# Whole-tile attention in three passes, 1e-9 on ScalarE, low weight halves on VectorE

## The chip, the cores and the metric

The kernel runs on one core of one Trainium2 chip. The core has five engines with a queue each: TensorE (PE in the profile, with its weight loads as PEld), VectorE (DVE), ScalarE (ACT), GpSimd (POOL) and SyncE (SP, which issues DMAs). An engine takes its instructions in the order in which they were written into its queue, and an instruction that waits holds those behind it. The metric is the device time of one execution in microseconds.

## What is computed

Three parts follow each other. Attention with a window: 4 batches, 8 heads, 768 positions, head size 64; a query in a chunk of 32 sees 16 positions to the left of the chunk, 8 to the right, and 8 memory positions. Then a gated product, and then a mix of 8 experts with balanced weights:

```python
scores = scale * np.matmul(q_c, k_full.transpose(0, 1, 3, 2))
scores = scores - np.max(scores, axis=-1, keepdims=True)
a = np.exp(scores)
a = a / (np.sum(a, axis=-1, keepdims=True) + 1e-09)
out[:, :, c_start:c_end] = np.matmul(a, v_full)
...
x = (x @ w_a) * (x @ w_b) @ w_out          # 3072 tokens, 512 -> 1536 -> 512
...
P = exp(logits - max); 8 times: rows, then columns of P scaled to sum 1 (columns to N / E)
for e in range(E):
    h = np.maximum(x @ w1[e], 0.0)
    out += P[:, e:e + 1] * (h @ w2[e])
```

## The kernel before, in words

**Precision.** A product is made of three: each operand is split into a high half (rounded to fp32r, by an ACT copy) and a low half (operand less high half). `mm3` multiplies low by high, high by low and high by high into one PSUM bank. Scores, transposes and values of attention are plain fp32 products; each of them stands in the trace with two records (of transposes, with one).

**First stage.** Tokens are in four passes of 768 (eight tiles of 96 queries), so a pass has 8 tiles of attention. A tile has two groups of four heads. For a group, `attn_group` adds: scores (PE, L408), masking with the scale (DVE, L417), negative maxima (DVE, L423), four exponentials with their sums (ACT, L426), the 1e-9 (DVE, L432), the reciprocal (DVE, L435), the product with it (POOL, L438, called the norm here), four transposes (PE, L445), a copy (ACT, L449), values (PE, L455), and the split of the result into `xbig` (ACT L463, DVE L466).

A pass has 12 steps of the gated product, two for each of six weight blocks: `product` makes `pab` (12 products of 128x384, L268), `second` makes `po` (6 of them). Attention of a pass is spread by its due times over the steps of the pass before; only the first pass's attention stands at the start with nothing beside it but the first weights. At the end of a pass come the logits: `pr`, a copy on ACT, and `folded` (`pl`).

**Weights.** Six blocks of six parts (128x512) are read in each of four passes, 144 parts in all. In the first pass the parts are made from 64-bit words on DVE (`d_clamp`, `d_shift`, `d_top`, `d_low`, L225 to L243). In every pass a part's high half is made by ACT (`w_high`, L257) and its low half by POOL (`w_low`, L261). Beside passes 2 to 4, weights of the expert stage are prepared: sums and splits on DVE in `dbuf`, `pbuf` and `xbig` (L277 in the trace, the helper `sub`), and stores from ACT's queue.

**The order.** `Order` holds a list of operations: engine, a cost, a due time, a function and what it comes after. `emit` runs them through a plan of its own: on each engine the ready operation with the lowest due time goes next, and the plan's times come from the costs. An engine name `DVE+` and the engine `POOL` share one port in this plan, so they exclude each other there. The order in which `emit` calls the functions is the order in every queue; the chip does not change it.

**Second stage.** The experts, from about 770 us to the end, with an order made in the same way.

## Time and profile before

| what | value |
| --- | --- |
| median of 3 runs | 2655.18 us (2654.46 to 2659.0) |
| the profiled execution | 2651.62 us, span 2649.7 us |
| PE, PEld busy | 2599.3 us (98%), 2218.6 us (84%) |
| DVE, ACT, POOL busy | 2122.5 us (80%), 1059.4 us (40%), 449.4 us (17%) |
| first stage to 760 us: PE, DVE, ACT, POOL busy | 729.7, 581.2, 422.6, 283.1 us |

The span runs from the first to the last instruction. A busy share is a mean over stages with different limits. Matmuls are pipelined and their ends are modelled, so on PE the distance from start to start tells more than a duration. In a row of a timeline several equal instructions are merged (x12); a bracket gives the idle time in front of it and what ended it.

### The profile page before, as it was taken

How to read it: one execution, taken by the hardware profiler on the slowest of the kernel's cores; microseconds unless marked ns; L12 is line 12 of the kernel's file. 1: busy time of each engine (PE TensorE's matmuls, PEld its weight loads, DVE VectorE, ACT ScalarE, POOL GpSimd, SP SyncE). 2: the span in 40 equal slices, each digit the busy share in tenths (PEclk: the TensorE clock that was granted, in tenths of full speed). 3: DMA queues.
4: the chain of work that ended last, by engine and by line, in shares of the span. 5: the costliest groups of instructions: out<-in, count | busy, mean ns of one | idle time of the engine just before them, and what ended most of it. 6: DMA issues, size and time to landing. Idle time of an engine off the chain costs nothing.

```text
span 2649.7 us, 35892 instructions
## 1 busy us (share of the span) xinstructions
PE 2599.3 (98%) x13067; PEld 2218.6 (84%) x13067; DVE 2122.5 (80%) x3093; ACT 1059.4 (40%) x1922; POOL 449.4 (17%) x270
## 2 busy tenths in 40 slices
PE   6999999999999999999999999999999999999998
PEld 5899989999987888888877888888887888888887
DVE  8985777886758999999997687777789587777777
ACT  7654655555425333333333322222233332323222
POOL 4443433333304222222210000000000000000000
PEclk8999999999999999999999999999999999999999
DMA  7654778778554666666676766666676766666663
GB/s 242 204 179 132 280 250 292 249 253 326 195 175 160 219 216 232 226 232 212 237 268 196 210 200 203 203 201 199 194 216 213 222 200 201 201 192 202 202 187 112
DMA packets 224079, 565.05 MB, mean 213 GB/s; under 512 B 21232, under 2 KB 41712, under 8 KB 219808
## 3 DMA queue, kind: packets, MB, share of 16 engines
q1 hardware_dynamic: 190112, 445.31, 54.1%
q10 hardware_dynamic: 33792, 117.44, 11.6%
q8 instruction: 105, 1.72, 0.3%
q14 instruction: 70, 0.57, 0.1%
HBM read 423.12 MB, written 139.56 MB: 212 GB/s over the span
## 4 chain that ended last, share of the span: by engine, by line
PE 91%; DVE 5%; DMA 2%; issue 1%; ACT 1%; POOL 0%; SPq 0%; ACTq 0%; DVEq 0%; POOLq 0%
PE py L268 25%; PE pa L268 19%; PE px L268 14%; PE pab L268 14%; PE po L268 7%; PE pr L268 7%; DMA wc<-xbig 1%; PE s_ps L408 1%; DVE xbig L277 1%; PE o_ps L455 1%; DVE sums L277 1%; PE t_ps L445 1%; DVE raw_e L277 0%; DMA abuf<-in_kw 0%; DVE hb L277 0%
## 5 line engine op out<-in xcount | busy, mean ns | idle before, releaser
L268 PE MATMUL py<-xbig,wbig 128*128 128x512 f32 x3168 | 802.3, 391 | 7.8 <-DVE sums L277 4.1
L268 PEld LDWEIGHTS py<-xbig,wbig 128*128 128x128 f32 x3168 | 594.7, 188 | 136.8 <-DVE sums L277 7.7
L1015 ACT ACTIVATE xbig<-hb 128x1024 fp32r<-128x1024 f32 x336 | 356.1, 1061 | 635.8 <-PE py L268 467.0
L268 PE MATMUL pa<-xbig,wbig 128*128 128x512 f32 x2304 | 586.3, 390 | 0.3 <-DVE xbig L277 0.3
L268 PEld LDWEIGHTS pa<-xbig,wbig 128*128 128x128 f32 x2304 | 431.4, 188 | 90.0 <-DVE xbig L277 0.9
L277 DVE TENSOR_TENSOR xbig<-hb,xbig 128x1024 fp32r<-128x1024 f32 x336 | 414.1, 1234 | 92.0 <-ACT xbig L1015 91.8
L277 DVE TENSOR_TENSOR sums<-py,sums 128x512 f32<-128x512 f32 x495 | 339.2, 686 | 164.1 <-PE py L268 157.9
L268 PE MATMUL px<-xbig,wbig 128*128 128x512 f32 x1728 | 441.9, 391 | 1.8 <-DVE part L277 1.1
L268 PE MATMUL pab<-xbig,wbig 128*128 128x384 f32 x2304 | 439.5, 339 | 1.7 <-DVE lg L606 1.6
L268 PEld LDWEIGHTS pab<-xbig,wbig 128*128 128x128 f32 x2304 | 401.6, 189 | 10.0 <-issue 3.5
L268 PEld LDWEIGHTS px<-xbig,wbig 128*128 128x128 f32 x1728 | 322.9, 188 | 70.5 <-DVE part L277 4.2
L937 ACT ACTIVATE part<-pa 128x512 f32<-128x512 f32 x192 | 114.8, 598 | 389.2 <-PE pa L268 388.2
L277 POOL TENSOR_TENSOR wbig<-raw_e,wbig 128x768 fp32r<-128x768 f32 (+1 forms) x56 | 166.3, 2970 | 448.4 <-ACT wbig L293 326.8
L268 PE MATMUL po<-gh,wbig 128*128 128x384 f32 x768 | 233.4, 346 | 2.2 <-ACT acc L581 2.2
L277 DVE TENSOR_TENSOR hb<-hb,hb 128x1024 f32<-128x1024 f32 x192 | 232.1, 1217 | 1.0
L951 DVE SCALAR_TENSOR_TENSOR hb<-part,pb 128x512 f32<-128x512 f32 x276 | 224.0, 815 | 2.6
L268 PE MATMUL pr<-xbig,wbig 128*128 128x512 f32 x864 | 218.8, 391 | 0.0
L268 PEld LDWEIGHTS pr<-xbig,wbig 128*128 128x128 f32 x864 | 162.9, 189 | 33.8
L277 DVE TENSOR_TENSOR part<-px,part 128x512 f32<-128x512 f32 x192 | 131.8, 686 | 38.7 <-PE px L268 36.0
L261 POOL TENSOR_TENSOR wbig<-raw_e,wbig 128x512 fp32r<-128x512 f32 x96 | 133.1, 1405 | 110.4 <-ACT wbig L257 102.4
L268 PEld LDWEIGHTS po<-gh,wbig 128*128 128x128 f32 x768 | 142.0, 189 | 8.3 <-ACT acc L581 2.4
L583 DVE TENSOR_TENSOR acc<-po,acc 128x384 f32<-128x384 f32 x160 | 88.7, 554 | 65.6 <-PE po L268 64.8
(126 smaller groups left out, 2157.5 us busy)
## 6 DMA issues: line engine op xcount, KB each, us to landing
wbig<-wc SPq DMA_DIRECT2D x336, 512.0 KB, 3.9
wbig<-wc SPq DMA_DIRECT2D x476, 256.0 KB, 3.5
wc<-xbig ACTq DMA_DIRECT2D x36, 1792.0 KB, 8.4
wc<-wbig ACTq DMA_DIRECT2D x28, 1792.0 KB, 7.7
raw_e<-w_f SPq DMA_DIRECT2D x72, 256.0 KB, 5.7
raw_e<-in_w_ex SPq DMA_DIRECT2D x28, 512.0 KB, 5.0
pb<-pT SPq DMA_DIRECT2D x23, 512.0 KB, 5.7
dbuf<-in_w_moe SPq DMA_DIRECT2D x18, 512.0 KB, 4.6
```

The source lines that it names most:

```text
L261: nc.gpsimd.tensor_tensor(out=wl, in0=raw(part), in1=f32(wh), op=ALU.subtract)
L268: nc.tensor.matmul(out=out, lhsT=a, rhs=b, start=first and i + j == 0, stop=last and i == n - 1 and j == 2, skip_group_check=skip,)
L277: (engine or nc.vector).tensor_tensor(out=out, in0=a, in1=b, op=op)
L408: nc.tensor.matmul(out=s_banks[:TQ, j % 2, 2 * g + j // 2, :], lhsT=qps[i % NQ][a:a + 64, (h0 + j) // 2, :], rhs=kts[i][a:a + 64, (h0 + j) ...
L445: nc.tensor.transpose(r["t_ps"][:, j, :], r["s"][:, j, :], ident[:TQ, :TQ])
L455: nc.tensor.matmul(out=r["o_ps"][a:a + 64, j // 2, :], lhsT=vts[i][:, h0 + j, :], rhs=r["pt"][:, 2 * (j % 2) + j // 2, :], start=True, sto ...
L583: nc.vector.tensor_tensor(out=a, in0=r["o", d], in1=a, op=ALU.add)
L937: "ACT", 0.6, at + 0.05, lambda: nc.scalar.activation(out=parts[j], in_=src, func=AF.Copy),
L951: y = add("DVE", 0.69, due, lambda: nc.vector.scalar_tensor_tensor(out=dst, in0=src, scalar=0.0, in1=pb[:, j * HB:(j + 1) * HB], op0=ALU.m ...
L1015: "ACT", 1.05, d, lambda: nc.scalar.activation(out=h, in_=src, func=AF.Copy), *deps, *t_used.get(t_n - NTR, ()))
```

## The change

Four edits. `w_low` moves from GpSimd to VectorE. The addition of 1e-9 moves from VectorE to ScalarE, as an activation with a bias from a small tile (`tiny`). Attention of passes 2 to 4 (24 tiles) is no longer by groups but by `attn_tile`: scores of all eight heads at once, one addition and one reciprocal for eight heads, one PSUM tile and one split for the values of eight heads, and values of a tile in one operation (`both`) with the scores of the next tile; only the last tile of a pass has values alone. And the folded logits get a later due time and their copy a higher cost in the plan.

```diff
@@ -137,6 +137,7 @@
     st1 = const.tile([P, E], F32, name="st1")
     mrow = const.tile([1, P], F32, name="mrow")
     mx = const.tile([P, 1], F32, name="mx")
+    tiny = const.tile([P, 1], F32, name="tiny")
 
     gate = const.tile([P, KT, 32], F32, name="gate")
     fold = const.tile([P, E], F32, name="fold")
@@ -258,7 +259,7 @@
 
     def w_low(i, part):
         wh, wl = w_halves(i, part)
-        nc.gpsimd.tensor_tensor(out=wl, in0=raw(part), in1=f32(wh), op=ALU.subtract)
+        nc.vector.tensor_tensor(out=wl, in0=raw(part), in1=f32(wh), op=ALU.subtract)
 
     def mm3(out, pairs, first=True, last=True, skip=False):
 
@@ -429,7 +430,7 @@
                 )
 
             def sums():
-                nc.vector.tensor_scalar_add(r["sm"], r["sm"], 1.0e-9)
+                nc.scalar.activation(out=r["sm"], in_=r["sm"], func=AF.Identity, bias=tiny[:TQ])
 
             def inverses():
                 nc.vector.reciprocal(r["sm"], r["sm"])
@@ -468,7 +469,7 @@
             scored[x] = add("PE", 0.6, due, scores, qk_loaded, scored.get(x - 1), taken.get(x - 2))
             taken[x] = y = add("DVE", 0.6, due, masked, scored[x], turned.get(x - 4))
             y = add("DVE", 0.6, due, maxima, y)
-            y = add("DVE+", 0.07, due, sums, *[add("ACT", 0.39, due, lambda j=j: exps(j), y) for j in range(4)])
+            y = add("ACT", 0.2, due, sums, *[add("ACT", 0.39, due, lambda j=j: exps(j), y) for j in range(4)])
             y = add("DVE", 0.1, due, inverses, y)
             y = add("POOL", 1.02, due, norm, y)
             turned[x] = add("PE", 0.34, due, transposes, y, turned.get(x - 1), copied.get(x - 1))
@@ -477,6 +478,118 @@
             y = highs_x[x] = add("ACT", 0.22, due, high, valued[x])
             settled[x] = add("DVE", 0.28, due, low, y)
 
+        held = []
+
+        def attn_tile(i, qk_loaded, v_loaded, due):
+            t = i % NT
+            mask = masks[0 if t == 0 else 2 if t == NT - 1 else 1]
+            x = 2 * i
+            r = {}
+
+            def scores():
+                for g in range(2):
+                    for j in range(4):
+                        a = 64 * (j % 2)
+                        nc.tensor.matmul(
...
+            def masked(g):
...
+            def sums():
+                nc.scalar.activation(out=r["sm"], in_=r["sm"], func=AF.Identity, bias=tiny[:TQ])
+
+            def inverses():
+                nc.vector.reciprocal(r["sm"], r["sm"])
+
+            def norm(g):
...
+            def values():
...
+            def settle():
+                y = highs_x[x] = highs_x[x + 1] = add("ACT", 0.42, due, high, valued[x])
+                settled[x] = settled[x + 1] = add("DVE", 0.47, due, low, y)
+
+            before = [scored[x - 1], taken[x - 2], taken[x - 1], qk_loaded]
+            if held:
+                values_before, settle_before, v_before = held.pop()
+
+                def both():
+                    values_before()
+                    scores()
+
+                y = add("PE", 2.1, due, both, *before, copied[x - 2], copied[x - 1], v_before, settled[x - 3])
+                valued[x - 2] = valued[x - 1] = y
+                settle_before()
+            else:
+                y = add("PE", 1.2, due, scores, *before)
+            scored[x] = scored[x + 1] = y
+            done = []
+            for g in range(2):
+                y = taken[x + g] = add("DVE", 0.6, due, lambda g=g: masked(g), scored[x], turned[x + g - 4], turned[x - 3])
+                y = add("DVE", 0.6, due, lambda g=g: maxima(g), y)
+                done += [add("ACT", 0.39, due, lambda g=g, j=j: exps(g, j), y) for j in range(4)]
+            y = add("ACT", 0.2, due, sums, *done)
+            y = inverted = add("DVE", 0.1, due, inverses, y)
+            for g in range(2):
+                y = add("POOL", 1.02, due, lambda g=g: norm(g), inverted)
+                turned[x + g] = add(
+                    "PE", 0.34, due, lambda g=g: transposes(g), y, turned[x + g - 1], copied[x + g - 1])
+                copied[x + g] = add("ACT", 0.55, due, lambda g=g: copies(g), turned[x + g], valued[x + g - 2] if x + g - 2 in valued else None)
+            if (i + 1) % TILES_A_PASS:
+                held.append((values, settle, v_loaded))
+            else:
+                valued[x] = valued[x + 1] = add(
+                    "PE", 0.95, due, values, copied[x], copied[x + 1], v_loaded, settled[x - 1])
+                settle()
+
+        TILES_A_PASS = SB // TQ
         GB = 2 * NB // TQ
         qk_in, v_in = {}, {}
         for x in range(2 * len(tiles)):
@@ -491,7 +604,10 @@
             if g == 0:
                 qk_in[i] = add("SP", 1.5, due - EARLY, lambda i=i: qk_load(i), scored.get(x - 2 * NQ + 1))
                 v_in[i] = add("SP", 0.5, due - EARLY + 0.1, lambda i=i: v_load(i), valued.get(x - 2 * NV + 1))
-            attn_group(x, i, g, qk_in[i], v_in[i], due)
+            if i < TILES_A_PASS:
+                attn_group(x, i, g, qk_in[i], v_in[i], due)
+            elif g == 0:
+                attn_tile(i, qk_in[i], v_in[i], due)
 
 
         highs, lows, stored, first_used, second_used = {}, {}, {}, {}, {}
@@ -520,7 +636,7 @@
 
                 used = (first_used if p * DN < n_parts(i) * DN - NF * D else second_used).get(i - 2, ())
                 highs[i, p] = add("ACT", 0.52, due, lambda p=p: w_high(i, p), y, *used)
-                lows[i, p] = add("POOL", 1.23, due, lambda p=p: w_low(i, p), highs[i, p], *used)
+                lows[i, p] = add("DVE+", 0.6, due, lambda p=p: w_low(i, p), highs[i, p], *used)
 
         gated = add("SP", 0.5, 4.0, lambda: nc.sync.dma_start(
             out=gate[:, :, 0:E], in_=w_gate.rearrange("(k p) e -> p k e", p=P)))
@@ -642,9 +758,9 @@
                 y = z = add("PE", 0.7, x + 1, logits, *seconds[-1:], *free_po[-2:-1], *mine, gated)
                 finished[n, k] = (stored_x[n, k], y)
                 seconds.append(y)
-                y = add("ACT", 0.4, x + 1, rows_copy, y)
+                y = add("ACT", 0.6, x + 1, rows_copy, y)
                 free_po.append(y)
-                y = add("PE", 0.6, x + 1, folded, *free_po[-2:-1], y)
+                y = add("PE", 0.6, x + 1.6, folded, *free_po[-2:-1], y)
                 seconds.append(y)
                 z = add("DVE", 0.15, x + 1, lg_copy, y)
                 free_po.append(z)
@@ -709,6 +825,7 @@
                     nc.vector.memset(halves[32 * c:32 * c + 32, :, lo:hi], 0.0)
             make_identity(nc, ident)
             nc.vector.memset(ones, 1.0)
+            nc.vector.memset(tiny, 1.0e-9)
 
             nc.vector.memset(gate, 0.0)
             nc.vector.reduce_sum(
```

The order of PE in the second pass. `o_ps` are values, `s_ps` scores, `t_ps` transposes, x4 four heads; `pab` and `po` are the gated product. Before:

```order
L268 MATMUL pab<-xbig,wbig 128x384 x12
L455 MATMUL o_ps<-pt,abuf 64x96 x4
L268 MATMUL po<-gh,wbig 128x384
L268 MATMUL po<-gl,wbig 128x384
L268 MATMUL po<-gh,wbig 128x384 x2
L268 MATMUL po<-gl,wbig 128x384
L268 MATMUL po<-gh,wbig 128x384
L408 MATMUL s_ps<-abuf 96x128 x4
L268 MATMUL pab<-xbig,wbig 128x384 x12
L445 MATMUL t_ps<-ident,s_sb 128x96 x4
```

After, the same engine in the same pass:

```order
L269 MATMUL pab<-xbig,wbig 128x384 x12
L531 MATMUL t_ps<-ident,s_sb 128x96 x4
L269 MATMUL po<-gh,wbig 128x384
L269 MATMUL po<-gl,wbig 128x384
L269 MATMUL po<-gh,wbig 128x384 x2
L269 MATMUL po<-gl,wbig 128x384
L269 MATMUL po<-gh,wbig 128x384
L269 MATMUL pab<-xbig,wbig 128x384 x12
L542 MATMUL o_ps<-pt,abuf 64x96 x8
L493 MATMUL s_ps<-abuf 96x128 x8
```

Values of four heads and scores of four heads were two visits; values of one tile and scores of the next, eight heads each, are now one.

The order of POOL at the start, norms (`s_sb`) and low halves (`wbig`). Before:

```order
L438 TENSOR_TENSOR s_sb<-s_sb,sm 96x512 x4
L261 TENSOR_TENSOR wbig<-raw_e,wbig 128x512
L438 TENSOR_TENSOR s_sb<-s_sb,sm 96x512
L261 TENSOR_TENSOR wbig<-raw_e,wbig 128x512
L438 TENSOR_TENSOR s_sb<-s_sb,sm 96x512
L261 TENSOR_TENSOR wbig<-raw_e,wbig 128x512 x2
L438 TENSOR_TENSOR s_sb<-s_sb,sm 96x512 x2
```

After:

```order
masks.py:199 AFFINE_SELECT ident<-ident 128x128
L439 TENSOR_TENSOR s_sb<-s_sb,sm 96x512 x16
L524 TENSOR_TENSOR s_sb<-s_sb,sm_896 96x512 x2
L524 TENSOR_TENSOR s_sb<-s_sb,sm_1135 96x512 x2
L524 TENSOR_TENSOR s_sb<-s_sb,sm_1388 96x512 x2
```

POOL's queue of the first stage holds norms alone now: 16 of the first pass, then two for each tile.

The order of DVE in the start: maskings (L417, after: L418), maxima (L423, L424), the 1e-9 (L432, gone), reciprocals (L435, L436), the making of the weights, the split of attention (L466, L467). Before:

```order
L229 TENSOR_SCALAR raw_e<-raw_e 128x512
L435 RECIPROCAL sm<-sm 96x4
L236 SCALAR_TENSOR_TENSOR raw_e<-dbuf,raw_e 128x512
L432 TENSOR_SCALAR sm<-sm 96x4
L435 RECIPROCAL sm<-sm 96x4
L243 SCALAR_TENSOR_TENSOR raw_e<-dbuf,raw_e 128x512
L466 TENSOR_TENSOR xbig<-o_ps,xbig 128x2x96
L432 TENSOR_SCALAR sm<-sm 96x4
L435 RECIPROCAL sm<-sm 96x4
L417 SCALAR_TENSOR_TENSOR s_sb<-s_ps,abuf 96x512
```

After:

```order
L230 TENSOR_SCALAR raw_e<-raw_e 128x512
L436 RECIPROCAL sm<-sm 96x4
L237 SCALAR_TENSOR_TENSOR raw_e<-dbuf,raw_e 128x512
L244 SCALAR_TENSOR_TENSOR raw_e<-dbuf,raw_e 128x512
L436 RECIPROCAL sm<-sm 96x4
L467 TENSOR_TENSOR xbig<-o_ps,xbig 128x2x96
L262 TENSOR_TENSOR wbig<-raw_e,wbig 128x512
L418 SCALAR_TENSOR_TENSOR s_sb<-s_ps,abuf 96x512
```

The additions left the queue, and a low half (L262) stands in it, in front of a masking.

## Rows read from the trace of the kernel before

**Rows 1.** Busy time by stretches: from:to, length, busy us (count) by engine, clock, DMA.

```profile
47.00:75.00 28.00, 25.23 (x209) 21.36 (x208) 27.29 (x60) 24.44 (x87) 13.44 (x11) 0.98 0.78 245
75.00:350.00 275.00, 275.00 (x1844) 254.79 (x1843) 211.12 (x418) 156.13 (x439) 111.91 (x84) 1.00 0.61 202
...
sum 760.00, PE 729.67 PEld 679.43 DVE 581.23 ACT 422.57 POOL 283.05; mean PE 72.97 PEld 67.94 DVE 58.12 ACT 42.26 POOL 28.30
```

**Rows 2.** Waits of PE, 75 to 760 us: who for whom, us, times, longest.

```profile
PE o_ps L455 <- ACT pt L449: 3.0, 2, 2.5
PE po L268 <- ACT acc L581: 2.2, 1, 2.2
PE pab L268 <- DVE lg L606: 1.6, 1, 1.6
PE po L268 <- DVE gl L568: 0.7, 1, 0.7
```

**Rows 3.** Timeline of PE, two visits of attention: start, us, what.

```profile
336.33 2.25 PE L268 MATMUL pab<-xbig,wbig 128*128 128x384 f32 x12
338.41 0.49 PE L445 MATMUL t_ps<-ident,s_sb 96*128 96x96 f32 x4
338.69 0.42 PE L268 MATMUL po<-gh,wbig 128*128 128x384 f32 x1
338.94 0.34 PE L268 MATMUL po<-gl,wbig 128*128 128x384 f32 x1
...
339.64 0.34 PE L268 MATMUL po<-gh,wbig 128*128 128x384 f32 x1
339.91 0.68 PE L408 MATMUL s_ps<-abuf 64*96 64x128 f32 x8
340.52 0.55 PE L455 MATMUL o_ps<-pt,abuf 128*64 128x96 f32 x8
341.00 2.35 PE L268 MATMUL pab<-xbig,wbig 128*128 128x384 f32 x12
343.19 0.33 PE L268 MATMUL po<-gh,wbig 128*128 128x384 f32 x1
```

**Rows 4.** The stretch 25 to 50 us, and scores of eight and four heads in it.

```profile
25.00:50.00 25.00, 16.58 (x114) 12.77 (x114) 22.39 (x50) 19.13 (x70) 14.63 (x11) 0.59 0.68 222
...
28.84 2.03 PE L408 MATMUL s_ps<-abuf 64*96 64x128 f32 x16
...
32.30 1.17 PE L408 MATMUL s_ps<-abuf 64*96 64x128 f32 x8
```

**Rows 5.** Busy time by stretches of the low halves (L261) alone.

```profile
0.00:75.00 75.00, 14.35 (x11) 0.86 0.76 243
...
sum 760.00, POOL 200.22; mean POOL 100.11
```

**Rows 6.** DVE to 760 us: groups (busy, mean ns), lines L568 and L277 (min/median/max).

```profile
L568 DVE TENSOR_TENSOR gl<-a_sb,gh 128x384 fp32r<-128x384 f32 x94 | 67.1, 717 | 13.1 <-ACT gh L565 12.8
L277 DVE TENSOR_TENSOR xbig<-dbuf,xbig 128x512 fp32r<-128x512 f32 x54 | 44.6, 843 | 6.0 <-ACT xbig L293 5.9
...
L568 DVE TENSOR_TENSOR gl<-a_sb,gh x94: 519/552/4064, 62.8 to 748.5; 128x384 fp32r<-128x384 f32 x94
...
L277 DVE TENSOR_TENSOR xbig<-dbuf,xbig x74: 410/680/1809, 254.6 to 730.3; 128x512 fp32r<-128x512 f32 x54, 128x256 fp32r<-128x256 f32 x18, 128x1024 fp32r<-128x1024 f32 x2
```

**Rows 7.** Busy time by stretches of the 1e-9 (L432) alone.

```profile
0.00:75.00 75.00, 5.03 (x17) 0.86 0.76 243
75.00:760.00 685.00, 10.23 (x48) 1.00 0.66 228
```

**Rows 8.** ACT to 760 us, groups of the exponentials.

```profile
L426 ACT ACTIVATE s_sb<-s_sb,nm 96x128 f32<-96x128 f32 x256 | 99.5, 391 | 42.1 <-DVE nm L423 42.1
...
L426 ACT ACTIVATION_READ_ACCUMULATOR s_sb<-s_sb,nm 96x1 f32 x256 | 48.3, 189 | 0.0
```

**Rows 9.** Idle time of PE in front of the values (L455), by what ended it.

```profile
  ACT pt L449: 13.0, 12
```

More of the change, by code (lines that the diff above doesn't have):

```diff
@@ L478, in attn_group, with maxima, exps, transposes @@
             settled[x] = add("DVE", 0.28, due, low, y)
+        held = []
[9 more added lines that the diff above has]
+                        nc.tensor.matmul(
+                            out=s_banks[:TQ, j % 2, 2 * g + j // 2, :], lhsT=qps[i % NQ][a:a + 64, (4 * g + j) // 2, :],
+                            rhs=kts[i][a:a + 64, (4 * g + j) // 2, :], start=True, stop=True,
+                        )
+            def masked(g):
+                if g == 0:
+                    r["nm"] = sp.tile([TQ, 8], F32, tag="nm8", name="nm8", bufs=2)
+                    r["sm"] = sp.tile([TQ, 8], F32, tag="sm8", name="sm8", bufs=2)
+                s = r["s", g] = sp.tile([TQ, 4, TK], F32, tag="s_sb", name="s_sb", bufs=4)
+                nc.vector.scalar_tensor_tensor(
+                    out=s.rearrange("p (b r) k -> p b (r k)", b=2),
+                    in0=s_banks[:TQ, :, 2 * g:2 * g + 2, :].rearrange("p b r k -> p b (r k)"), scalar=SCALE,
+                    in1=mask[:, None, :].to_broadcast([TQ, 2, 2 * TK]), op0=ALU.mult, op1=ALU.add,
+                )
+            def maxima(g):
+                nc.vector.tensor_reduce(out=r["nm"][:, 4 * g:4 * g + 4], in_=r["s", g], axis=AX.X, op=ALU.max, negate=True)
+            def exps(g, j):
+                s = r["s", g][:, j, :]
+                c = 4 * g + j
+                nc.scalar.activation(out=s, in_=s, func=AF.Exp, bias=r["nm"][:, c:c + 1], accum_out=r["sm"][:, c:c + 1])
+            def sums():
[3 more added lines that the diff above has]
+            def norm(g):
+                nc.gpsimd.tensor_tensor(
+                    out=r["s", g], in0=r["s", g], in1=r["sm"][:, 4 * g:4 * g + 4, None].to_broadcast([TQ, 4, TK]), op=ALU.mult
+                )
+            def transposes(g):
+                r["t", g] = ps.tile([P, 4, TQ], F32, tag="t", name="t_ps")
+                for j in range(4):
+                    nc.tensor.transpose(r["t", g][:, j, :], r["s", g][:, j, :], ident[:TQ, :TQ])
+            def copies(g):
+                r["pt", g] = sp.tile([P, 4, TQ], F32, tag="pt", name="pt", bufs=2)
+                nc.scalar.activation(out=r["pt", g], in_=r["t", g], func=AF.Copy)
+            def values():
+                r["o"] = ps.tile([P, 4, TQ], F32, tag="o", name="o_ps")
+                for g in range(2):
+                    for j in range(4):
+                        a = 64 * (j % 2)
+                        nc.tensor.matmul(
+                            out=r["o"][a:a + 64, 2 * g + j // 2, :], lhsT=vts[i][:, 4 * g + j, :],
+                            rhs=r["pt", g][:, 2 * (j % 2) + j // 2, :], start=True, stop=True,
+                        )
+            here_h, here_l = (x1(y, slice(0, 4), i * TQ, TQ) for y in range(2))
+            def high():
+                nc.scalar.activation(out=here_h, in_=r["o"], func=AF.Copy)
+            def low():
+                nc.vector.tensor_tensor(out=here_l, in0=r["o"], in1=f32(here_h), op=ALU.subtract)
+            def settle():
[20 more added lines that the diff above has]
+            y = inverted = add("DVE", 0.1, due, inverses, y)
+            for g in range(2):
+                y = add("POOL", 1.02, due, lambda g=g: norm(g), inverted)
[8 more added lines that the diff above has]
+                settle()
```

## The prediction

> **What bounds the kernel now.** I read the busy time by stretches first, then the waits of PE, then PE's timeline, and last the groups of DVE and POOL. The stretches [rows 1] show a start in which DVE is close to full (27.3 of 28.0 us between 47 and 75), and behind it a stretch in which PE is busy without a gap (275.0 of 275.0) while DVE has 211 and ACT 156. The reader should not trust a busy PE alone, since its ends are modelled; so the second view is what PE waited for between 75 and 760 us, nearly the end of the first stage [rows 2]. It is 7.5 us in all, in five waits: 3.0 for the copies of attention, 2.2 for a copy of a sum, 1.6 for the logits and 0.7 for a split. So in this stage the time is the sum of what PE is given, and whatever is taken from PE's queue shortens the run as long as nothing new makes PE wait. All that the change touches lies there; the expert stage behind it issues the same work.
>
> The third view is how PE's queue runs through a visit of attention, from start to start [rows 3]. Twelve undisturbed products of `pab` take 338.41 - 336.33 = 2.08 us, so 0.17 each. Transposes of four heads take 0.28 us (338.41 to 338.69), and the product behind them 0.25 instead of 0.17: 0.08 more. In the next visit, scores and values: the last `po` before it takes 0.27 instead of 0.17 (339.64 to 339.91), scores of four heads 0.61, values of four heads 0.48, and the twelve `pab` behind 2.19 instead of 2.08. Going into and coming out of such a visit thus costs 0.10 + 0.11 = 0.21 us beyond its content, however much is in it.
>
> **The change, part by part.**
>
> *Attention by whole tiles, on PE.* In the built orders of PE I counted the unbroken runs of attention or logits products between expert products, from the first `pab` on: 133 before, 92 after. Those with scores or values in them fall from 89 to 33, those of transposes alone rise from 34 to 48. The number of products is the same. Switching: 56 x 0.21 = 11.8 us less, 14 x 0.08 = 1.1 us more, so 10.7 us less. Inside the runs there is a second gain: 24 have scores of eight heads and 25 values of eight heads. No row shows eight heads at the full clock, but the start has both lengths of scores where the granted clock is near the lower level (0.59 on the mean of its stretch) [rows 4]: the second four heads add 2.03 - 1.17 = 0.86 us. At twice the clock that is 0.43 instead of 0.61, so 0.18 x 24 = 4.3 us. For the values I take the same ratio, 0.70 of 0.48, so 0.14 x 25 = 3.5 us. The ends of this part: nothing for the longer runs (10.7 us in all), or the values gain as much as the scores (0.18 each, 19.5 us). I take 10.7 + 4.3 + 3.5 = 18.5 us, since rows 4 are the only ones of that length.
>
> By the Trainium skill, page TensorEngine Tiling (Array Packing), section Tiling Modes, a change of tiling mode, not only of the tile, drains TensorE, and the turn from values to scores inside the new visit is such a change. If it cost another 0.10 us there, the sum would be some 2 us smaller. The turn from scores to values in rows 3 lies within the 0.61 us, so the trace speaks for leaving it out.
>
> *The low halves of the weights, from POOL to DVE.* There are 144, and they take 200.2 us of POOL, 1.39 each [rows 5]. On DVE the nearest row is the same subtraction in the same shapes for the expert weights: mean 843 ns, median 680 [rows 6]. The mean lies over the median because some run to 1.8 us, and for `gl` to 4.1 us; such a long one holds PE in the 0.7 us of rows 2. I read these as DVE losing time beside POOL. Mean less median, times count: `gl` 94 x 0.165 = 15.5 us, `xbig<-dbuf` 54 x 0.163 = 8.8, so 24 us in two groups of many. Of POOL's 283.1 us the low halves are 71%, so at least 17 us of these two go. Added: 144 x 0.68 = 98 us. Gone from DVE besides: the 1e-9, 15.3 us [rows 7], and in 24 tiles one of two reciprocals and part of a split (an estimate of 8 us). Net at most 98 - 17 - 15 - 8 = +58 us; at the other end each low half frees as much of DVE as it adds, and the net is 23 us less. Even at the worst DVE goes from 581 to 639 of 760 us. It lies beside PE: between 75 and 350 us DVE has 64 us free. I put nothing on PE for it, and take off the 0.7 us for `gl`. If this cover is gone, it is in the start. What queues behind: a low half waits for ACT's high half and holds DVE's queue until then, as it now holds POOL's, where the norms stand behind it.
>
> *The start.* Eleven low halves stood in the first 75 us on POOL: 11 x 0.68 = 7.5 us more on DVE, 5.0 us of 1e-9 less [rows 5, 7], and relief between 17/144 = 0.12 and 0.68 us for each low half, 1 to 7.5 us. That is +1 to -5, or +4.3 with the 0.843 of the mean and no relief. I take 0.
>
> *The 1e-9 on ACT.* 40 small instructions, 16 by group and 24 by tile. The nearest row is the reading of an accumulator, 189 ns [rows 8]: 7.6 us on an engine busy 423 of 760. In the chain it takes the place of a DVE instruction of 15.3/64 = 0.24 us. Nothing, between -1 and +1.
>
> *The later due time of the folded logits.* It puts more in front of them; 1.6 us were waited for them in one place. I take 1 us less, between 0 and 1.6.
>
> *New waits.* PE's order now holds values of one tile and scores of the next as one block. If the values are late, the scores and all expert products behind wait too. Between this block and the first transposes of the next tile stand three `po` and three `pab`, 3 x 1.04 + 3 x 2.08 = 9.4 us. The tile's chain in that time: two maskings and two maxima of 0.68 like the row of that length, of which two are ahead of the first exponential (1.4 us), eight exponentials of at most 0.39 + 0.19 (4.6), the addition and the reciprocal 0.2 each, the norm (283.1 - 200.2)/64 = 1.3: 7.7 us. So 1.7 us are left for other work in the queues of DVE and ACT. I take 2 us of waits over all tiles; the ends are 0 and 26 (below).
>
> *Sum.* -18.5 - 0.7 - 1 + 2 = -18.2 us. On the profiled execution, 2651.62 us with a span of 2649.7, that is 2633.4. It lies 3.6 us under the median of the runs shown (2655.18), and I put the difference on the median: 2637 us.
>
> **The rivals.**
>
> *The block waits (slower).* Between a tile's last copy and its values. When PE waited for such a copy it was 12 times and 13.0 us, 1.1 us each [rows 9], most of it in the start. If each of the 24 tiles does so once, 26 us come in place of the 2 I took: 2637 + 24 = 2661 us. It decides from 25.5 us over 24 tiles, 1.06 us a tile (18.2 + 2 + the 5.3 us of 0.2%). For it: the slack of 1.7 us, and ACT's queue that held the copies up to 3.0 us in two places. Against it: only these two waits are left after 75 us [rows 2], in an order packed as closely.
>
> *Only the switches are saved.* The long runs cost what two short ones do, and the start is 4.3 us longer: 2655.2 - 10.7 + 4.3 - 1.7 + 2 = 2649 us; without the longer start 2645. For it: no row of eight heads at the full clock, and DVE without room in the start. Against it: rows 4, and the relief.
>
> *The gain goes into waits for ACT.* ACT's copies held PE 3.0 + 2.2 us in three places [rows 2]. A tile's chain is now longer and may meet every such hold: with five more of 3 us each, 2637 + 15 = 2652 us. Against it: nothing in the change makes ACT later but 7.6 us of small instructions.
>
> **How the numbers follow.** The forecast has 0.64, the switches alone 0.18, the block that waits 0.10, the holds of ACT 0.08. The forecast's own range is 2631 to 2643: 5 us better in the start and 1 of waits less, or 6 us of the long runs not there. The range for 8 of 10 goes down to 2630 and up to 2650, past the switches alone. A change within 0.2% (5.3 us, 2649.9 to 2660.5) is about what cannot be told from none. Faster: the forecast, the switches alone nearly whole, and a third of the holds, 0.84. Within 0.2%: the rest of these and a third of the waiting block, 0.08. Slower: 0.08.
>
> **What would show it.** In PE's timeline a visit of values and scores of eight heads each takes 0.34 + 0.48 + 0.43 + 0.61 = 1.9 us and 0.21 beyond; at 2.4 in all the longer runs gain nothing. The first stage ends some 18 us earlier with PE as full as before. On DVE the low halves take 0.68 us, and `gl` and the splits have means near their medians. PE's waits behind 75 us stay under 10 us. I am wrong if values or transposes stand high among them, if DVE fills the first 200 us and PE waits for its splits, or if the start is over 4 us longer.

## The result and the profile after

| | before | after |
| --- | --- | --- |
| median of the comparison | 2657.09 us (2654.46 to 2661.84) | 2625.54 us (2624.67 to 2630.01) |
| ratio, 95% interval | | 0.9888 (0.9876 to 0.99) |
| a second comparison | 2656.23 us | 2626.89 us, 0.9894 (0.9879 to 0.9909) |
| profiled execution, span | 2651.62, 2649.7 us | 2624.67, 2622.9 us |

The change is faster by 26.9 us in the profiled pair and by 28 to 32 us in the comparisons (by ratios and by medians). The forecast was 2637 us with a range down to 2630: the direction was right, the gain was half as large again as the 18.2 us of the forecast, or more.

The busy time by stretches of the changed kernel answers to [rows 1] (from:to, length, busy us and count by engine, clock, DMA):

```profile
47.00:75.00 28.00, 24.87 (x203) 21.35 (x202) 25.48 (x57) 23.55 (x85) 8.95 (x6) 1.00 0.77 244
75.00:350.00 275.00, 273.12 (x1892) 262.87 (x1892) 226.74 (x439) 164.05 (x462) 33.97 (x28) 1.00 0.63 209
0.00:735.00 735.00, 714.10 (x4781) 682.40 (x4782) 590.50 (x1163) 425.83 (x1146) 83.74 (x70) 1.00 0.70 237
```

The stage that [rows 1] sum over 760 us now takes some 733. PE is as full as it was, POOL has 84 us to do instead of 283. The surprise is DVE: 144 more low halves, and 590.5 us of work where 581.2 stood.

The waits of PE from 75 to 735 us, against [rows 2]:

```profile
PE t_ps L531 <- POOL s_sb L524: 2.6, 2, 1.9
PE pab L269 <- DVE a_sb L675: 0.6, 1, 0.6
```

The waits in all four lines of [rows 2] are gone; in their place stand two of transposes for a norm and a short one for DVE.

A visit of values and scores on PE's timeline, against [rows 3]:

```profile
206.75 1.55 PE L269 MATMUL pab<-xbig,wbig 128*128 128x384 f32 x8
208.23 0.88 PE L542 MATMUL o_ps<-pt,abuf 128*64 128x96 f32 x16
209.04 1.12 PE L493 MATMUL s_ps<-abuf 64*96 64x128 f32 x16
210.09 0.44 PE L269 MATMUL po<-gh,wbig 128*128 128x384 f32 x1
210.37 0.33 PE L269 MATMUL po<-gl,wbig 128*128 128x384 f32 x1
```

Values 0.81 us from start to start, scores 1.05, the product behind them 0.28 instead of 0.17. With the product ahead, which is 0.10 longer, the visit costs 2.06 us beyond its neighbours, and 21 such visits lie within 0.01 us of that. The turn from values to scores costs nothing that can be seen.

DVE by groups, 0 to 735 us, against [rows 5, 6] (busy us, mean ns | idle before):

```profile
L262 DVE TENSOR_TENSOR wbig<-raw_e,wbig 128x512 fp32r<-128x512 f32 x96 | 67.1, 711 | 1.4 <-ACT wbig L258 1.4
L684 DVE TENSOR_TENSOR gl<-a_sb,gh 128x384 fp32r<-128x384 f32 x94 | 55.2, 596 | 7.5 <-ACT gh L681 7.5
L278 DVE TENSOR_TENSOR xbig<-dbuf,xbig 128x512 fp32r<-128x512 f32 x54 | 37.8, 725 | 6.5 <-ACT xbig L294 6.5
L278 DVE TENSOR_TENSOR pbuf<-pbuf 128x256 f32<-128x256 f32 x72 | 29.9, 428 | 2.2 <-DMA pbuf<-in_w_ex 2.2
```

`gl` has gone from 717 to 596 ns and `xbig<-dbuf` from 843 to 725; the sums in `pbuf`, which were 690 ns in the kernel before, are at 428. The low halves themselves take 0.71 us.

**Where the time went.** I split PE's time by the distances from start to start. *Visits*: everything between products of `pab` and `po`, and what the products at the edges take beyond 173.3 ns. *Waits*: idle time that ends with a release. *Slow products*: what products of `pab` and `po` away from a visit take beyond 173.3 ns, where that is over 57 ns (at the lower clock they take some 320). *Other products*: the rest, 3401 products. The first column reaches to the first `pab`, the last from the last `pab` to PE's end. The two executions of each kernel are different runs (the second ones belong to the experiments below).

| us | to first pab | visits | waits | slow products | other products | behind |
| --- | --- | --- | --- | --- | --- | --- |
| before | 47.2 | 106.8 | 10.3 | 3.7 | 590.5 | 1885.9 |
| before, second | 46.1 | 107.1 | 9.2 | 5.6 | 590.5 | 1890.5 |
| after | 44.0 | 87.4 | 6.4 | 1.4 | 593.2 | 1885.2 |
| after, second | 45.1 | 87.2 | 5.7 | 1.8 | 593.2 | 1887.4 |
| low halves on DVE alone | 41.9 | 107.0 | 5.6 | 1.8 | 590.4 | 1885.8 |
| the same, old order | 46.9 | 107.6 | 6.1 | 3.6 | 590.5 | 1888.0 |
| 1e-9 on ACT alone | 46.0 | 106.3 | 8.0 | 2.4 | 590.6 | 1887.3 |
| whole tiles alone | 47.5 | 90.1 | 16.8 | 8.4 | 593.8 | 1887.4 |
| after, low halves on POOL, new order | 44.3 | 87.9 | 9.5 | 6.1 | 593.2 | 1887.0 |
| after, a second subtraction on POOL | 45.2 | 94.4 | 43.8 | 13.0 | 593.1 | 1884.8 |
| after without tiles | 43.1 | 106.1 | 2.1 | 1.6 | 590.7 | 1883.6 |
| after, 1e-9 on DVE | 46.1 | 88.8 | 4.0 | 2.0 | 594.0 | 1887.9 |
| after, tiles in the first pass too | 74.0 | 94.4 | 18.8 | 4.7 | 593.0 | 1884.2 |
| after, 1e-9 on DVE in tiles only | 43.3 | 86.8 | 3.1 | 0.9 | 593.2 | 1887.6 |

### The profile page after: what moved, and what is told of

The parts are those of the page before. It is cut to its first block, busy times and chain, and to the rows that moved or that the text cites. A ratio compares the mean times of both kernels' runs of the same rounds, so it can differ in the third digit from the quotient of the medians.

```text
span 2622.9 us, 35569 instructions
## 1 busy us (share of the span) xinstructions
PE 2581.8 (98%) x13067; PEld 2219.2 (85%) x13067; DVE 2134.1 (81%) x3126; ACT 1060.2 (40%) x1938; POOL 245.4 (9%) x126
## 4 chain that ended last, share of the span: by engine, by line
PE 87%; DVE 9%; DMA 2%; issue 1%; ACT 1%; POOL 0%; SPq 0%; ACTq 0%; DVEq 0%; POOLq 0%
PE py L269 24%; PE pa L269 18%; PE pab L269 14%; PE px L269 14%; PE po L269 7%; PE pr L269 6%; DVE xbig L278 2%; DVE sums L278 2%; DVE hb L1068 1%; DMA wc<-xbig 1%; DVE raw_e L278 1%; PE s_ps L493 1%; DVE hb L278 1%; PE o_ps L542 1%; DMA raw_e<-in_w_ex 1%
## 5 line engine op out<-in xcount | busy, mean ns | idle before, releaser
L269 PE MATMUL pab<-xbig,wbig 128*128 128x384 f32 x2304 | 433.6, 336 | 0.7 <-DVE a_sb L675 0.6
L1068 DVE SCALAR_TENSOR_TENSOR hb<-part,pb 128x512 f32<-128x512 f32 x276 | 233.9, 851 | 2.6
L269 PE MATMUL po<-gl,wbig 128*128 128x384 f32 x384 | 129.5, 337 | 0.0
```

The source lines that it names most:

```text
L269: nc.tensor.matmul(out=out, lhsT=a, rhs=b, start=first and i + j == 0, stop=last and i == n - 1 and j == 2, skip_group_check=skip,)
L1068: y = add("DVE", 0.69, due, lambda: nc.vector.scalar_tensor_tensor(out=dst, in0=src, scalar=0.0, in1=pb[:, j * HB:(j + 1) * HB], op0=ALU.m ...
```

## The experiments

Theory A: what the forecast missed is the time that DVE lost beside POOL, and with it waits of PE and a lower clock behind them. Theory B: the order that the plan made, or another edit, did it. Distances to the changed kernel are between medians of different comparisons; by the ratios to the kernel before, those of the slower variants are up to 3 us larger.

**Low halves on DVE, alone** (the kernel before with one edit).

```diff
-        nc.gpsimd.tensor_tensor(out=wl, in0=raw(part), in1=f32(wh), op=ALU.subtract)
+        nc.vector.tensor_tensor(out=wl, in0=raw(part), in1=f32(wh), op=ALU.subtract)
-                lows[i, p] = add("POOL", 1.23, due, lambda p=p: w_low(i, p), highs[i, p], *used)
+                lows[i, p] = add("DVE+", 0.6, due, lambda p=p: w_low(i, p), highs[i, p], *used)
```

> The kernel before with one edit: the 144 low halves on VectorE, attention still by groups. Theory A (VectorE no longer runs beside GpSimd's subtractions, so its own instructions get shorter and the start and the waits shrink): 8 to 11 us faster than before, the 96th product of pab near 80 us instead of 86.2, gl's mean near 0.60 us instead of 0.717, PE's waits from 75 us on near 4 us instead of 8.8, the visits of attention unchanged at 98 us. Theory B (start and waits got shorter by the new order of attention or by the 1e-9, not by the low halves): no gain, or up to 4 us slower in the start, since VectorE has 98 us more to do.

Measured: 2644.11 us against 2655.43, ratio 0.9959 (0.9947 to 0.9971), some 11 us. The waits of PE from 75 to 748 us:

```profile
PE pab L268 <- ACT a_sb L556: 0.2, 1, 0.2
PE t_ps L445 <- POOL s_sb L438: 0.2, 1, 0.2
```

The total is theory A's: an edit on which I had put 0.7 us is worth 11, with the order that the plan makes for it. In the table the first product comes 5.3 us earlier, with one group of scores and one of transposes fewer ahead of it; the waits are 4.7 us less, the slow products 1.9. The 97th `pab` (the expectations, which count from 0, call it the 96th) comes 3.2 us earlier, at 83.0 and not near 80. The waits in all four lines of [rows 2] went, those for ACT's copies too.

**The same in the old order.** Only the engine of the instruction is changed; the plan still books POOL, and PE, ACT and SP run the rows of the kernel before.

```diff
-        nc.gpsimd.tensor_tensor(out=wl, in0=raw(part), in1=f32(wh), op=ALU.subtract)
+        nc.vector.tensor_tensor(out=wl, in0=raw(part), in1=f32(wh), op=ALU.subtract)
```

> The kernel before with its order kept on TensorE, ScalarE and SyncE; the 144 low halves leave GpSimd's queue and stand in VectorE's at the places that the order gives them. Nothing else changes, and the plan still counts them as GpSimd's. Theory A (the engine alone, without a new order, takes away the waits and the lower clock behind them): the waits from the 96th product of pab on fall from 7.5 us to under 2, the products at the lower clock from 3.2 us to under 1, and 6 to 10 us are gained in all. A rival (the gain of the edit is the new order): within 3 us of before, or slower, since the plan puts VectorE's other work where it believes VectorE to be free.

Measured: 2646.18 us against 2655.21, ratio 0.997 (0.9961 to 0.998), 8 us. By these figures the engine alone brings most of the 11, though the two intervals overlap. Behind the 97th `pab` the slow products fall from 3.2 to 0.7 us as expected (in the whole table they stay, 3.6), the waits from 7.5 to 3.4, not to under 2:

```profile
PE o_ps L455 <- ACT pt L449: 2.2, 2, 1.7
PE po L268 <- ACT acc L581: 0.9, 2, 0.7
PE pab L268 <- ACT a_sb L556: 0.4, 1, 0.4
```

Against [rows 2] the waits named after DVE are gone (2.3 us). Those named after ACT's copies in `pt` and `acc` fell from 5.2 to 3.1, but `pt` alone (2.2) not below the 2.0 of the second execution of the kernel before. The first product stays where it was (46.9); the start's gain of the run above came with the new order. The profiled execution is the slowest of nine (2649.91), so its rows show less of the gain than the ratio: 1.7 us between the profiled pair, 4.2 of waits less and 2.1 more behind the last `pab`.

The waits for ACT's copies have a further link, which ACT's timeline of the kernel before shows:

```profile
383.61 0.84 ACT L293 ACTIVATE xbig<-dbuf 128x768 fp32r<-128x768 f32 x1 [4.44 <-DMA wc<-xbig]
385.52 0.48 ACT L449 ACTIVATE pt<-t_ps 128x384 f32<-128x384 f32 x1
...
458.77 0.84 ACT L293 ACTIVATE xbig<-dbuf 128x768 fp32r<-128x768 f32 x1 [5.02 <-DMA wc<-xbig]
459.52 0.47 ACT L581 ACTIVATE acc<-po 128x384 f32<-128x384 f32 x1
```

ACT stood idle 4.44 and 5.02 us until a store of expert weights (`wc<-xbig`) had landed, and the copies, for which PE waited 2.51 and 2.22 us, stood in its queue behind that. DVE (3.35 and 4.34 us) and POOL were idle there too, so these two waits are not time that DVE lost beside POOL at that place. ACT still stands idle for such stores in this run and in the changed kernel, up to 4.2 us; in the changed kernel no wait of PE between 75 and 735 us is named after ACT.

**The 1e-9 on ACT, alone.**

```diff
-                nc.vector.tensor_scalar_add(r["sm"], r["sm"], 1.0e-9)
+                nc.scalar.activation(out=r["sm"], in_=r["sm"], func=AF.Identity, bias=tiny[:TQ])
```

> The kernel before with one edit: the 1e-9 on ScalarE. Theory A: within 1.5 us of before, the start unchanged (96th product of pab at 85 to 87 us). Theory B, in the form that the 1e-9 made the start long: 4 to 7 us faster, with the 96th product near 80 us.

Measured: 2651.87 us, ratio 0.9986 (0.9978 to 0.9995), 3.6 us: more than the 1.5 of theory A, and not in the start, against theory B (its 97th `pab` stands at 87.7 us, before at 86.2). Waits are 2.3 us less.

**Whole tiles, alone.**

```diff
-            attn_group(x, i, g, qk_in[i], v_in[i], due)
+            if i < TILES_A_PASS:
+                attn_group(x, i, g, qk_in[i], v_in[i], due)
+            elif g == 0:
+                attn_tile(i, qk_in[i], v_in[i], due)
```

> The kernel before with one edit: attention of the last three passes by whole tiles, low halves on GpSimd, the 1e-9 on VectorE. Theory A: the visits from 75 us on fall by 18 us (98.5 to 80), the start stays (96th product of pab at 85 to 87 us), PE's waits stay at 7 us or more because long GpSimd instructions stand in front of the norms: 14 to 18 us faster than before. Theory B (the new order of attention shortens the start and the waits as well): 22 to 28 us faster, as much as the whole change.

Measured: 2652.6 us, ratio 0.9989 (0.998 to 0.9999): 3 us. Both expectations failed. The visits fell as they should, by 16.7 us; 6.5 us of waits, 4.7 of slow products and 3.3 of other products took them back. The waits of PE from 75 to 755 us:

```profile
PE po L268 <- DVE gl L683: 6.3, 3, 3.3
PE pab L268 <- DVE a_sb L674: 5.3, 3, 2.5
PE pab L268 <- ACT a_sb L671: 1.0, 2, 0.7
PE po L268 <- ACT acc L696: 1.0, 1, 1.0
PE t_ps L530 <- POOL s_sb L523: 1.0, 3, 0.5
```

One of them on the timelines of DVE, POOL and PE:

```profile
362.49 4.06 DVE L683 TENSOR_TENSOR gl<-a_sb,gh 128x384 fp32r<-128x384 f32 x1 [0.70 <-ACT gh L680]
...
361.20 2.49 POOL L523 TENSOR_TENSOR s_sb<-s_sb,sm 96x512 f32<-96x512 f32 x2
363.65 4.03 POOL L261 TENSOR_TENSOR wbig<-raw_e,wbig 128x512 fp32r<-128x512 f32 x3
...
366.60 0.69 PE L268 MATMUL po<-gl,wbig 128*128 128x384 f32 x1 [2.59 <-DVE gl L683]
367.09 0.52 PE L268 MATMUL po<-gh,wbig 128*128 128x384 f32 x1
367.41 2.90 PE L268 MATMUL pab<-xbig,wbig 128*128 128x384 f32 x9
```

A `gl` of 0.55 us takes 4.06 while POOL runs two norms and three low halves without a gap; PE waits 2.59 us for it. A tile gives POOL two norms at once, so that such rows of POOL get longer. And the products behind the wait take 0.32 us instead of 0.17. Busy time by stretches of that place shows the granted clock (seventh number):

```profile
363.00:367.00 4.00, 1.41 (x9) 1.09 (x8) 4.00 (x2) 0.82 (x2) 4.00 (x4) 0.94 1.02 339
367.00:371.00 4.00, 4.00 (x19) 3.96 (x18) 2.58 (x6) 0.59 (x2) 0.69 (x1) 0.63 0.71 260
371.00:375.00 4.00, 4.00 (x37) 3.75 (x34) 2.70 (x7) 1.83 (x4) 0.00 (x0) 1.00 0.63 240
```

PE worked 1.41 of 4 us, then had the lower of its two clocks (1.2 instead of 2.4 GHz) for a part of the next 4, then the full one. So a wait of 2.6 us cost 1.8 us more behind it: eleven products there are 0.16 us too long each.

**The changed kernel with the low halves on POOL, in the new order.**

```diff
-        nc.vector.tensor_tensor(out=wl, in0=raw(part), in1=f32(wh), op=ALU.subtract)
+        nc.gpsimd.tensor_tensor(out=wl, in0=raw(part), in1=f32(wh), op=ALU.subtract)
```

> The changed kernel, its order kept on every engine, with the low halves executed by GpSimd again: they leave VectorE's queue and stand in GpSimd's at the places that the order gives them. Theory A: 7 to 12 us slower than the changed kernel (15 to 20 us faster than before): gl's mean back over 0.68 us, the 96th product of pab 4 us or more later, waits for norms or splits longer. A rival (the order that the new plan made is what shortened the start, the engine that executes the low halves does not matter): within 2 us of the changed kernel, although VectorE has 100 us less to do.

Measured: 2634.74 us, 9.2 above the changed kernel; ratio to before 0.9925 (0.9913 to 0.9938), some 20 us faster than before. Theory A's 7 to 12 held; the 97th `pab` came 2.4 us later (82.2), not 4. In the table the waits are 3.1 us more than in the changed kernel, the slow products 4.7. The waits of PE from 75 to 735 us:

```profile
PE t_ps L531 <- POOL s_sb L524: 2.5, 3, 1.2
PE po L269 <- DVE gl L684: 2.0, 2, 1.6
PE pab L269 <- DVE a_sb L675: 1.8, 1, 1.8
```

Those for norms are what they were (2.6 us in the changed kernel), although the low halves stand in POOL's queue again; what is new are 3.8 us for DVE's `gl` and `a_sb`. So here the cost comes over DVE. Its groups of DVE:

```profile
L684 DVE TENSOR_TENSOR gl<-a_sb,gh 128x384 fp32r<-128x384 f32 x96 | 84.2, 885 | 21.8 <-ACT gh L681 21.4
L278 DVE TENSOR_TENSOR xbig<-dbuf,xbig 128x512 fp32r<-128x512 f32 x54 | 46.4, 885 | 7.5 <-ACT xbig L294 7.5
```

And the busy time of the first 740 us, first of this kernel, then of the changed one:

```profile
0.00:740.00 740.00, 713.05 (x4760) 680.33 (x4761) 592.92 (x1016) 423.49 (x1144) 277.73 (x214) 0.98 0.69 235
```

```profile
0.00:740.00 740.00, 718.52 (x4805) 685.31 (x4805) 593.47 (x1168) 426.32 (x1147) 83.74 (x70) 1.00 0.70 238
```

DVE is busy 592.9 us without the low halves and 593.5 us with them: what it does more, it does in the time that it lost beside POOL.

Theory B has its part too. This kernel and the one with whole tiles alone both have tiles, and low halves on POOL, and yet are 18 us apart (2634.74 and 2652.6). They differ in the engine of the 1e-9, in the due time of the logits, and in the order, which there books the low halves on POOL. Of this, the 1e-9 was worth 3.6 us in the kernel before; no run divides the rest.

**A second subtraction on POOL.** The changed kernel, its order on PE, DVE, ACT and SP kept; POOL does a copy of each low half's subtraction too, into a part of `xbig` that is filled later.

```diff
+                add("GHOST", 1.23, due, lambda p=p: w_ghost(i, p), highs[i, p])
```

> The changed kernel with its order kept on TensorE, VectorE, ScalarE and SyncE, and one thing added: GpSimd executes a copy of each low half's subtraction too, into a part of xbig that the expert stage fills later. VectorE does all that it did. Theory A (what a GpSimd subtraction costs is the time of the VectorE instructions beside it, and then the waits of TensorE and its lower clock behind a wait): 5 to 14 us slower than the changed kernel; gl's mean over 0.68 us instead of 0.60, stretches of products at the lower clock again, the 96th product of pab 2 to 5 us later, more than by leaving VectorE the low halves alone would explain. A rival (VectorE's queue holds enough air, and the gain came from the places that the order gave to the low halves): within 2 us. If the added waits are all of transposes for norms, GpSimd's queue and not VectorE is what it costs.

Measured: 2681.08 us, 55.5 above the changed kernel, ratio to before 1.0106 (1.0091 to 1.0122): four times the most that theory A gave. Both copies are released by the same high half and run against each other. DVE's groups, and behind them PE's longest waits:

```profile
L262 DVE TENSOR_TENSOR wbig<-raw_e,wbig 128x512 fp32r<-128x512 f32 x96 | 108.0, 1137 | 1.5 <-ACT wbig L258 1.4
L689 DVE TENSOR_TENSOR gl<-a_sb,gh 128x384 fp32r<-128x384 f32 x91 | 69.1, 767 | 9.7 <-ACT gh L686 9.3
```

```profile
PE t_ps L535 <- POOL s_sb L528: 18.4, 17, 2.5
PE pab L273 <- DVE a_sb L680: 6.1, 4, 4.9
```

The low half takes 1137 ns instead of 711, and `gl` 767 instead of 596; but the largest wait is for norms, that is for POOL's own queue. The cost of a POOL instruction has two parts, what it does to DVE beside it and what stands behind it in POOL's queue. This run does not divide them; in the run above only the first shows.

**The changed kernel without tiles** (`attn_group` in all passes).

> The changed kernel with attention by groups in all passes. Theory A: TensorE's visits of attention come back whole (92 us instead of 77 between the 96th product of pab and the end of the first stage), waits stay small since low halves are on VectorE: 13 to 17 us slower than the changed kernel. A rival (whole tiles also take load from VectorE, so that without them its splits come late): 18 to 25 us slower, with waits for gl or a_sb over 5 us.

Measured: 2636.42 us, 10.9 above the changed kernel, ratio to before 0.9939 (0.9927 to 0.9952). The visits came back (106.1 us), and no wait of PE is left from 75 us to the last `pab`. So tiles are worth 3 us alone, with the low halves and an order for them on POOL, and 11 to 13 us in the changed kernel, where theory A had 13 to 17.

**The changed kernel with the 1e-9 on DVE.**

> The changed kernel with the 1e-9 on VectorE again. Theory A (its gain alone was 3 to 4 us because VectorE ran beside GpSimd; with the low halves on VectorE it adds 40 instructions of 0.2 us and nothing waits for them): 0 to 3 us slower. A rival (the small instruction stands in VectorE's queue and waits there for the last exponential, so that splits behind it come late): 5 us or more slower, with PE's waits from 75 us on over 8 us.

Measured: 2627.93 us, 2.4 above the changed kernel, 0.9909 (0.9895 to 0.9923). The total is theory A's (by the ratios it is 5.6 us), the parts are not: the 97th `pab` comes 5.5 us later (85.3), and from there the stage is 2.9 us shorter. In the start the plan puts a masking behind weight pieces, and PE's scores wait for it:

```profile
39.49 1.17 PE L408 MATMUL s_ps<-abuf 64*96 64x128 f32 x8 [6.02 <-DVE s_sb L417]
```

**Tiles in the first pass too.**

```diff
-            if i < TILES_A_PASS:
-                attn_group(x, i, g, qk_in[i], v_in[i], due)
-            elif g == 0:
+            if g == 0:
                 attn_tile(i, qk_in[i], v_in[i], due)
```

> The changed kernel with attention of the first pass by whole tiles too. Theory A (VectorE bounds the start, and whole tiles have 8 reciprocals and 8 additions fewer and joint splits): the 96th product of pab 0 to 3 us earlier, 1 to 3 us faster in all. A rival (in the start nothing hides a tile's chain, eight exponentials stand ahead of its first norm, and the first product comes later): 2 to 6 us slower, the first pab later than 46 us.

Measured: 2676.48 us, 50.9 above the changed kernel, 1.0091 (1.0077 to 1.0105). The rival was right in kind and far too small. PE's largest wait from 0 to 75 us, and one tile on its timeline:

```profile
PE t_ps L531 <- POOL s_sb L524: 45.4, 8, 12.6
```

```profile
39.53 2.02 PE L493 MATMUL s_ps<-abuf 64*96 64x128 f32 x16
54.11 0.90 PE L531 MATMUL t_ps<-ident,s_sb 96*128 96x96 f32 x4 [12.55 <-POOL s_sb L524]
```

From a tile's scores to its first transposes are 14.6 us, and nothing lies beside them. In the last three passes products of `pab` and `po` do.

**The 1e-9 on ACT in the first pass, on DVE in the tiles.** It joins the start of the changed kernel to the rest of the run with the 1e-9 on DVE.

> The changed kernel with the 1e-9 on ScalarE in the first pass only and on VectorE in the tiles of the last three passes. With the 1e-9 on VectorE everywhere the start was 5.5 us longer and the rest of the first stage 2.9 us shorter than in the changed kernel. If the two come from their own passes, the 96th product of pab stands near 80 us, no wait is left behind it, and the kernel is 2 to 4 us faster than the changed one (some 29 to 33 us faster than before). If the start hangs on the whole order, which changes here too, it stays at 82 to 86 us and nothing is gained.

Measured: 2622.17 us, ratio to before 0.9879 (0.9862 to 0.9895). The 97th `pab` is at 78.5 us, and between 75 and 735 us no wait of PE is left.

**Second executions.** The kernel before, the changed kernel and the last variant, again.

> The kernel before, unchanged, profiled once more. If the terms belong to the kernels, its 96th product of pab stands at 85 to 88 us, the waits behind it are 6 to 9 us, the products at the lower clock 2 to 4 us, the visits 92 us. If they belong to the execution, one of them moves by half of its difference or more (start under 83 us, waits and lower clock together under 7 us).

> The changed kernel, profiled and timed once more. If the terms belong to the kernels: the 96th product of pab at 79 to 81 us, waits of 2 to 4 us, nearly nothing at the lower clock, visits of 77 us, some 30 us faster than before. If they belong to the execution: a start of 83 us or more, or waits and lower clock together over 7 us.

> The changed kernel with the 1e-9 on ScalarE in the first pass and on VectorE in the tiles, beside the changed kernel on one chip. If the one wait for a norm (2.6 us) is what it takes away, it is 2 to 4 us faster; if that wait belongs to the execution, both are within 1 us of each other.

Measured: 2656.08, 2626.89 and 2623.21 us; the last two on the same chip, ratios to before 0.9894 (0.9879 to 0.9909) and 0.988 (0.9864 to 0.9897). In the kernel before the four lines of [rows 2] come back by name, with 2.0, 2.4, 1.6 and 0.7 us, the longest for `pt` at another visit (1.6 us at 375.7 instead of 2.5 at 386.1). In the table the visits repeat to 0.3 us, waits to 1.1, slow products to 1.9, the first product to 1.1 (97th `pab`: 86.2 and 87.2 before, 79.8 and 81.2 after). So visits, waits and the 97th `pab` belong to the kernels. The slow products and the first product move by up to 1.9 and 1.1 us between two executions of one kernel, and fall by 2.3 to 3.8 and 1.0 to 3.2 between the two kernels, so their sizes are less sure. What lies behind the last `pab`, the same work in all, moves by 4.6 us between executions of one kernel. The variant with the 1e-9 split has the lowest medians; of its 3.4 and 3.7 us over the changed kernel the intervals of the ratios overlap, so that gain is likely and not shown.

## Why the forecast was too small

| term, us | forecast | first pair | second pair |
| --- | --- | --- | --- |
| visits | -18.5 | -19.4 | -19.9 |
| waits (gl, logits, new ones) | +0.3 | -3.9 | -3.5 |
| slow products (clock) | none | -2.3 | -3.8 |
| start, to the first pab | 0 | -3.2 | -1.0 |
| other products | none | +2.7 | +2.7 |
| behind the last pab | 0 | -0.7 | -3.1 |
| sum | -18.2 | -26.8 | -28.6 |

*What bounds the kernel* was right: PE stayed full, and what left its queue shortened the run.

*Whole tiles on PE* was right in mechanism and size. The joint visit was put at 1.9 and 0.21 us, 2.07 to 2.1, and measured 2.06. The longer runs did gain at the full clock. Of the 19.4 us, 15.2 lie behind the 97th `pab`, although four groups of scores, one of values and two of transposes more stand there than before.

*The low halves* is the step that failed: "I put nothing on PE for it, and take off the 0.7 us for `gl`". I had read in [rows 6] that DVE loses time beside POOL, and bounded DVE's net work by -23 and +58 us; +9 came (0.6 in a fixed order). But I gave PE only the one wait that carried the name of `gl`. In the changed kernel's order the engine of the low halves is worth 9.2 us, and everything else in the change, this order with it, some 20, where 17.5 were forecast. Alone the edit is worth 11 us with a new order and 8 in the old one. What the runs with tiles and low halves on POOL show in the place of that step: beside a full queue of POOL a `gl` or an addition of DVE can last 4 to 6 us, PE waits for it or for what stands behind it on DVE, and behind some of these waits products run at the lower clock. For the two longest waits of [rows 2] this path is not shown. The prediction took the link in their names, ACT's copies, for the cause, and behind that link is a store; why they went with the low halves on DVE in a new order stays open.

*New waits* were sized right, 2 us taken and 2.6 us there (1.9 in the second execution), waits for norms, in the chain that the prediction gave 1.7 us of slack. The wait of the blocking rival, values that wait for their copy, shows in no run behind 75 us in which the last three passes alone have tiles. Whole tiles alone did give back 14.5 of their 16.7 us, but in waits for DVE's `gl` and `a_sb`, at the lower clock and in the other products.

*Slow products* were not in the sum at all. In the kernel before 2.6 of their 3.7 us stand behind the two longest waits, in 18 products of mostly 0.32 us. *Other products* take 0.8 ns longer each (174.4 against 173.6) in every kernel with tiles and in none without; the runs don't say why.

*The start* was forecast at 0 between +4.3 and -5, and 3.2 and 1.0 us came, inside these ends. It hangs on the plan: between 41.9 and 47.5 us to the first product in the kernels with groups there, with no rule by edit.

*The 1e-9* was 0 within 1; it is 3.6 us alone and 2.4 in the changed kernel, and on DVE in the tiles, on ACT before them, the medians are lower still. *The folded logits*: their wait is gone in the run of the low halves alone too, so this edit need not have done it. It was not run by itself.

## What to carry to other kernels

Where means of DVE instructions lie above their medians while GpSimd works, count all that time as lost on DVE and look for what waits behind it. Follow a wait back beyond the engine that its name gives: here two of them led past ACT to a store. Edits don't add: three of them gave 11, 4 and 3 us alone and 29 together (with a fourth that was not timed by itself), since what the longer runs on PE save can go into waits, as in whole tiles alone. Price a wait of PE with what follows it: here one of 2.6 us cost 1.8 us more at the lower clock, while those of the changed kernel, none over 1.9 us, cost next to nothing. The length alone does not tell: with the low halves on POOL in the new order, a wait of 1.80 us has eleven products of 0.29 to 0.32 us behind it, 1.6 us more, at a granted clock of 0.65 over the 4 us there.

## What the hardware showed

DVE can be kept out for several GpSimd instructions in a row. In the run with whole tiles alone, DVE and POOL:

```profile
258.88 6.22 DVE L277 TENSOR_TENSOR pbuf<-pbuf 128x256 f32<-128x256 f32 x1
...
256.92 2.93 POOL L523 TENSOR_TENSOR s_sb<-s_sb,sm 96x512 f32<-96x512 f32 x2
259.81 1.28 POOL L261 TENSOR_TENSOR wbig<-raw_m,wbig 128x512 fp32r<-128x512 f32 x1
261.05 3.76 POOL L261 TENSOR_TENSOR wbig<-raw_e,wbig 128x512 fp32r<-128x512 f32 x3
```

An addition of 0.42 us lasted 6.22 us, until the last of five gapless GpSimd instructions was done or nearly. Held were the forms that read two operands from SBUF (`pbuf` up to 6.22 us here, `gl` to 5.08 with the low halves on POOL in the new order, integer pieces of the weights to 3.68 in the run of the 1e-9 alone) and some that read one (a clamp of the weights 2.26 us instead of 0.42, a 1e-9 1.29 instead of 0.16, both here). Those with an operand in PSUM never were (`a_sb` at most 0.56 us, the maskings 0.69), nor the maxima (0.68).

The Trainium skill, page SBUF — State Buffer, section SBUF: two separate sides, states that the two engines share a port pair under an exclusive lock, taken for a whole instruction by whichever starts first, among others by a DVE instruction with two SBUF inputs against a GpSimd one that reads SBUF. The traces agree for two operands in SBUF against one of them in PSUM (6.22 against 0.56 us). By it alone one would look for a wait of one GpSimd instruction at most, and the row shows five.
